# Two attentions on one core: A's first block's chain four steps sooner, exponents beside products, first scores ahead, ten block sums copied by VectorE

## The chip, the cores and the metric

The kernel runs on one core of one Trainium2 chip. The metric is the device time of one execution in microseconds. Engines are called by the names of the profile: PE is TensorE's matmul and PEld its weight load, DVE is VectorE, ACT is ScalarE, POOL is GpSimd, SP is SyncE, which issues most DMAs.

## The reference

Two attention layers with 32 heads of 18 over 2048 positions of width 576, each with its own input and weights; their outputs stand side by side.

```python
qkv = (x @ wqkv).reshape(B, S, 3, H, Dh)            # B, S, D = 1, 2048, 576; H = 32; Dh = 18
# A: each position sees the 8 positions 0, 2, .. 14 before it (masked below zero)
idx = pos[:, None] - arange(8)[None, :] * 2
logits = einsum("bhsd,bhswd->bhsw", q, kg) * scale; logits = where(mask, logits, -1e9)
a = einsum("bhsw,bhswd->bhsd", softmax(logits), vg)
# B: full attention
p = softmax(einsum("bhqd,bhkd->bhqk", q, k) * scale)
b = einsum("bhqk,bhkd->bhqd", p, v)
out = concatenate([a_heads @ wo_A, b_heads @ wo_B], axis=-1)
```

## The kernel before

**Ahead of the steps** (up to some 413 us) the inputs are split into a rounded part and a rest, so that products of 32-bit numbers can be made of rounded ones, and q, k and v of both layers are projected and stored.

**The steps.** B's attention runs in 512 steps, 8 groups of four heads (`g`) by 4 blocks of 512 queries (`b`) by 16 tiles of 128 keys (`kt`). A block thus has 16 steps, and its first has `kt == 0`. A step makes four scores of 128 keys by 512 queries (`score`, L263) into banks of the ring "scores"; ScalarE takes their exponentials (`e`, L268). The four `e` of the step before are then weighed with `v` into the bank `po` (`weigh`, L731), which also sums the denominators. The numbers of a step in the text are counted from 0.

**The maxima.** Exponentials need a bound for each query. It is found ahead of time for later blocks: query-key products of half the partitions, 512 wide (`maximum`, `take`, L160), each reduced by VectorE out of its bank (`reduce`, L168). In each step there are two whole ones and one that consists of two halves of 256 (`parts_of_maximum`: its first matmul, then, after a `nop` of ScalarE, its second). All of these use the three banks of the ring "else". `given` counts what has been handed out and `total` what there is. When all is given, the kernel goes over to weighing two steps together (`paired`).

**Row halves.** Scores and maxima use 54 to 56 of the 64 rows of one half of TensorE's array, so a score in one half runs beside a maximum in the other. The loop at the end writes the order out: first part, score 0, whole, score 2, score 1, second part, score 3, whole.

**The end of a block.** The weighing of `kt == 15` is made in the next block's first step. `finish` (L740) then copies `po` into `o`, and the next weighing waits for that copy. Normalising goes through small DMAs and GpSimd (L767 to L769) and is planned 1 to 26 steps later.

**A's attention** is made by GpSimd and VectorE beside this, in eight blocks of 256 positions, one each 54 steps (`local`, `GAP`, `A_FROM`). `plan` puts a function on the agenda of a step, and `due` emits it at that step's end. An engine runs its own queue in that order, as soon as the operands are there, so GpSimd may run ahead of or behind the step. The chain of a block: fetch q and k, `match` (GpSimd, L868 to L875, logits `lg`), `most` (VectorE, L886, three steps), `lower` (L892), `exponents` (ScalarE, L895), `total` and `inverses` (VectorE, L886 and L902), `share` (L905), `weighted` (L911 to L914), `upper`, `rest`, `put` to memory, `get` back transposed.

**A's output products.** Four for each block (`sums_of_a`, L1036): `MADE` holds the steps at whose end they are put into `inside`, and the next step makes one ahead of its last score, with two maxima woven in. ScalarE then copies one half out of its bank (L954) and VectorE adds the other (L955).

**B's output products** come at the end, in group 7 (`sum_of`, L1036, with L1055 and L1056 on VectorE). While more than four pieces of maxima are due they run inside a step like A's; later they run as `waiting` between the scores and the weighing. `producing` holds the steps with products of either kind.

**GpSimd's other work** in its queue: splitting the bounds (L103, L104 with `mh`, `mt`) and the output weights (L103, L104 with `wohi`, `wolo`), the latter three steps after each of five loads at steps 28 to 44.

Of the kernel before, what the change touches and what calls it, by code (L numbers as in the profile page):

```python
# [10 lines left out]
AF = mybir.ActivationFunctionType  # L11
# [8 lines left out]
DH = 18  # L20
# [22 lines left out]
GAP = 54  # L43

A_FROM = 10

MADE = ((88, 96, 112, 128), (144, 160, 176, 192), (201, 208, 224, 240), (250, 256, 272, 288),
        (304, 320, 336, 352), (361, 368, 384, 400), (412, 416, 432, 448), (466, 468, 475, 480))


def ap(t, *dims):

    return bass.AP(tensor=t.tensor, offset=t.offset, ap=[list(t.ap[0])] + [list(d) for d in dims])
# [8 lines left out]
def two_attentions(ctx: ExitStack, tc, xa, wa, woa, xb, wb, wob, out):  # L62
# [5 lines left out]
    nc = tc.nc  # L68
# [28 lines left out]
    po = p_po.tile([128, 512], F32, name="po")  # L97
# [10 lines left out]
    step = 0  # L108
# [99 lines left out]
    given = [0, 0]  # L208
# [17 lines left out]
    begun = deque()  # L226
# [26 lines left out]
    e_room = None  # L253
    counted = [-1]

    def score(g, b, kt, h, kind="scores"):

        assert (g, b) in placed
        qs, ks = sets[g % 3]
        p, r = divmod(h, 2)  # L260
        ps = bank(kind)
        at = slice(64 * r, 64 * r + 56)
        nc.tensor.matmul(ps, ks[at, p, 128 * kt : 128 * kt + 128], qs[at, b, p], start=True, stop=True)  # L263

        counted[0] += 1
        early = counted[0] % 8 < 6
        e = (e_room if early else work).tile([128, 512], F32, name="e", bufs=6 if early else 2)
        nc.scalar.activation(e, ps, AF.Exp, scale=SCALE)  # L268
        return e
# [100 lines left out]
    with (tc.tile_pool(name="x", bufs=1, side="right") as xp,  # L370
# [103 lines left out]
        if True:  # L474
# [34 lines left out]
            for c in range(5):  # L509
                one, other = (load, nc.scalar.dma_start) if c % 2 == 0 else (nc.scalar.dma_start, load)  # L510
# [11 lines left out]
            ahead = deque()  # L522
# [188 lines left out]
            es = []  # L711
# [10 lines left out]
        step = 0  # L722
# [13 lines left out]
    def finish(g, b):  # L736
        o = work.tile([128, 512], F32, name="o", bufs=2)
        if g == NG - 1 and b == NB - 1:
            return closing(b, o, work.tile([128, 512], F32, name="rec", bufs=1))
        nc.scalar.activation(o, po, AF.Copy)  # L740
        den = work.tile([128, 16], F32, name="den", bufs=2)
        rec = work.tile([128, 512], F32, name="rec", bufs=1)
        parts = []

        def room():
            if g == NG - 1 and b == 0:

                parts[:] = [ap(work.tile([128, 4, 128], F32R, name=f"at{i}", bufs=1), (1, 512)) for i in range(2)]
            else:
                n = work.tile([128, 2, 512], F32R, name="n", bufs=1)  # L750
                parts[:] = n[:, 0], n[:, 1], n
            return parts

        if g == NG - 1 and b > 0:
            return shortly(b, o, rec, *room()[:2])

        def store():
            if g < NG - 1:
                load(do[:, g, :, 512 * b : 512 * b + 512].rearrange("i p n -> p i n"), parts[2].bitcast(F32))
            else:  # L760
                plan(step, full(b, parts))

        for at, f in ((1, lambda: load(den, o[DH:128:32])),
                      (8, lambda: nc.vector.reciprocal(den, den)),
                      (9, lambda: load(drec[g, b].rearrange("i (p n) -> (i p) n", n=16), den)),
                      (13, lambda: load(rec, rows(drec[g, b], (512, 4), (0, 32), (1, 512)))),
                      (18, lambda: nc.gpsimd.tensor_mul(o, o, rec)),  # L767
                      (19, lambda: nc.gpsimd.tensor_copy(room()[0], o)),
                      (20, lambda: nc.gpsimd.tensor_sub(parts[1], o, parts[0])),  # L769
                      (26, store)):  # L770
            later(at, f)
# [47 lines left out]
    wo = {}  # L819

    producing = set()

    def load_wo(k, src, *pieces):

# [20 lines left out]
    def local(j):  # L845
# [20 lines left out]
        def match(c):  # L866
            pr = wide()
            nc.gpsimd.tensor_mul(pr, ap(st["q"][:, 2 * c], (SUB, 2), (0, W), (1, SUB)), window(st["k"], c))  # L868
            if c == 0:
                st["pr"] = pr  # L870
            else:
                nc.gpsimd.tensor_add(st["pr"], st["pr"], pr)  # L872
            if c == DH // 2 - 1:
                lg = st["lg"] = work.tile([128, W, SUB], F32, name="lg", bufs=1)
                nc.gpsimd.tensor_add(lg, st["pr"][:, 0], st["pr"][:, 1])  # L875
                if j == 0:
                    for w in range(1, W):
                        nc.gpsimd.memset(lg[:32, w, : DIL * w], MASKED)
# [28 lines left out]
        def weighted(c):  # L907
            if c == 0:
                st["o"] = work.tile([128, DH, SUB], F32, name="ao", bufs=1)
            at = wide()  # L910
            nc.gpsimd.tensor_mul(at, ap(st["lg"], (0, 2), (SUB, W), (1, SUB)), window(st["v"], c))  # L911
            nc.gpsimd.tensor_add(at[:, :, :4], at[:, :, :4], at[:, :, 4:])  # L912
            nc.gpsimd.tensor_add(at[:, :, :2], at[:, :, :2], at[:, :, 2:4])  # L913
            nc.gpsimd.tensor_add(st["o"][:, 2 * c : 2 * c + 2], at[:, :, 0], at[:, :, 1])  # L914
# [10 lines left out]
        def put(i):  # L925
            load(rows(dao[j, i, 0, 0], (DH * SUB, 128), (1, DH * SUB)),
                 ap(st["parts"][i].bitcast(F32), (1, DH * SUB)))
# [18 lines left out]
        def sums_of_a(h):  # L946
            his, los = zip(*wo["a"])
            w = his[:4], los[:4], his[4], los[4]
            cols = slice(288 * h, 288 * h + 288)
            if h == 0:  # L950
                st["y"] = ys["a", j, st["n"]] = work.tile([128, D], F32, name="y", bufs=4)
            one, two = beside("scores", *(halves(r, 0, w, st["x"], cols, slice(0, 128), True) for r in range(2)))
            y = st["y"][:, cols]
            nc.scalar.activation(y, two, AF.Copy)  # L954
            behind_scores.append(lambda: nc.vector.tensor_add(y, one, y))  # L955

        pieces = [(33, lower), (35, exponents), (39, share), (60, upper), (61, rest), (64, lambda: put(0)), (66, lambda: put(1))]

        pieces[:0] = [(at, lambda f=f, n=n: f(n)) for f, ats in ((most, (31, 32, 33)), (total, (36, 37, 38)),
                                                                (inverses, (38, 39))) for n, at in enumerate(ats)]  # L960
        for c in range(DH // 2):
            pieces.append((5 + 5 * c // 2, lambda c=c: match(c)))
            pieces.append((39 + 5 * c // 2, lambda c=c: weighted(c)))

        for nm, at, apart in (("q", -18, 2), ("k", -10, 2)) if j else (("q", -9, 1), ("k", -5, 1)):
            pieces += [(at + apart * i, lambda nm=nm, i=i: fetch(nm, i)) for i in range(4)]
# [77 lines left out]
    def sum_of(y, t, h, chunks, kind=None):  # L1044

        pos, cols = slice(128 * t, 128 * t + 128), slice(288 * h, 288 * h + 288)
        both = []
        for r in range(2):
            both.append([])
            for c, (hi, lo) in enumerate(chunks):  # L1050
                at = slice(64 * r, min(64 * r + 64, hi.shape[0]))
                whi, wlo = wo["b"][c]
                both[r] += [(a[at, pos], w[at, cols]) for a, w in ((hi, whi), (hi, wlo), (lo, whi))]
        one, two = beside(kind, *both)
        nc.vector.tensor_copy(y, one)  # L1055
        nc.vector.tensor_add(y, two, y)  # L1056

    def first(t, b, h):
# [74 lines left out]
    rest = NG * NB * PIECES * 2 - early  # L1133

    total = early + rest
# [4 lines left out]
    while step < ALL:  # L1140
        n, kt = divmod(step, NT)
        g, b = divmod(n, NB)
        es = [None] * 4

        whole = total - sum(given) > 1
        parts = bool(begun) or total - sum(given) > 3

        ps = bank() if inside and whole else None
        if parts:
            part = parts_of_maximum()  # L1150
        for h in (0, 2, 1, 3):

            if inside and h == 3:
                inside.pop(0)()
            es[h] = score(g, b, kt, h)
            if h == 0 and whole:
                maximum(1, ps)()
            if h == 1 and parts:
                part()
            if h == 3 and whole:  # L1160
                maximum(0)()
        for fs in (behind_scores, outside):
            while fs:
                fs.pop(0)()

        paired = paired or kt % 2 == 0 and sum(given) == total and not begun
        for _ in range(1 if paired and step < ALL - 2 else len(waiting)):
            if waiting:
                waiting.pop(0)()
        if ready and (kt % 2 == 0 or not paired):  # L1170
            weigh(ready.pop(0))
        ready.append((g, b, kt, es))
        if paired and kt % 2:
            weigh(*ready)
            ready.clear()
        due()

        if len(waiting) > (0 if not paired else 2 if kt % 2 else len(waiting)):
            waiting.pop(0)()
        step += 1  # L1180
# [24 lines left out]
```

## Time and profile before

| | us |
|---|---|
| median of 3 runs | 1619.08 |
| lowest and highest run | 1617.21, 1622.39 |
| the profiled execution's own time | 1616.82 |
| its span, first to last instruction | 1615.0 |
| mean granted TensorE clock | 0.997 of full speed |

| engine | busy us | share of the span |
|---|---|---|
| PE | 1599.0 | 99% |
| PEld | 959.5 | 59% |
| DVE | 1393.9 | 86% |
| ACT | 1212.4 | 75% |
| POOL | 961.1 | 60% |

Times of rows in the trace count from the start of the span. A row names start, duration, engine, line and operation, then the tiles (out <- in), their shapes and how many instructions are merged into it. Square brackets hold the idle time of the engine before it and what ended that time. Matmuls are pipelined, and their modelled ends overlap, so a high share of PE does not say that its array is full.

### The profile page before, as it was taken

Reading aid. Unit: us, or ns where it says so; the run is one execution under the profiler, and the core shown is the slowest. Engines: PE = TensorE matmul, PEld = TensorE weight load, DVE = VectorE, ACT = ScalarE, POOL = GpSimd, SP = SyncE. Lnnn points to the kernel's source line nnn. Section 1 sums busy time; section 2 is a strip of 40 time slices with the busy share of each in tenths; the row PEclk is TensorE's granted clock in tenths of the full one; section 3 lists DMA queues with packets and bytes.
Section 4 is the critical chain, followed back from the end, with each engine's and each line's share of the span. In section 5 each row is a group of like instructions: output and inputs, shape, how many; then the busy total and the mean of one; then the engine's idle time right before and its main releaser. Section 6 shows DMA issues by size and latency. Waiting matters only on the chain.

```text
span 1615.0 us, 35230 instructions
## 1 busy us (share of the span) xinstructions
PE 1599.0 (99%) x13394; PEld 959.5 (59%) x13394; DVE 1393.9 (86%) x2366; ACT 1212.4 (75%) x2419; POOL 961.1 (60%) x792
## 2 busy tenths in 40 slices
PE   9999999999999999999999999999999999999998
PEld 7999888999544444444444444444444444445676
DVE  5199999999899998999999999999999999999532
ACT  6424442121799998999999999999999999998444
POOL 2405742210265995996995995995996997920000
PEclk9999999999999999999999999999999999999999
DMA  8937954432222262254235235332532241034201
GB/s 250 239 121 196 275 164 133 134 104 79 60 56 64 73 147 54 62 118 113 62 85 133 72 98 115 98 91 60 125 106 58 59 135 47 22 124 139 89 38 60
DMA packets 186058, 172.11 MB, mean 107 GB/s; under 512 B 119152, under 2 KB 132976, under 8 KB 184160
## 3 DMA queue, kind: packets, MB, share of 16 engines
q1 hardware_dynamic: 181024, 158.31, 35.3%
q0 software_dynamic: 4032, 10.63, 3.1%
q8 instruction: 105, 1.72, 0.5%
q10 hardware_dynamic: 832, 0.92, 0.2%
q14 instruction: 65, 0.53, 0.1%
HBM read 96.94 MB, written 71.90 MB: 105 GB/s over the span
## 4 chain that ended last, share of the span: by engine, by line
PE 82%; POOL 7%; DVE 5%; DMA 3%; ACT 2%; issue 1%; SPq 0%; POOLq 0%; DVEq 0%; ACTq 0%
PE po L731 24%; PE bank L160 15%; PE bank L353 15%; PE bank L263 15%; PE bank L1036 8%; PE bank L290 5%; DVE mx L168 4%; ACT e L268 2%; POOL pr L868 1%; POOL pr L872 1%; POOL pr L911 1%; DMA akv<-da 1%; DMA dqk<-olo 1%; POOL pr L912 1%; POOL pr L913 0%
## 5 line engine op out<-in xcount | busy, mean ns | idle before, releaser
L168 DVE TENSOR_REDUCE mx<-bank 128x2 f32<-128x512 f32 x2048 | 1286.0, 684 | 114.5 <-PE bank L160 86.2
L268 ACT ACTIVATE e<-bank 128x512 f32<-128x512 f32 x2048 | 1050.2, 607 | 90.3 <-PE bank L263 83.2
L160 PE MATMUL bank<-ks,qs 54*128 54x256 f32 (+1 forms) x2536 | 791.8, 377 | 7.4 <-DVE mx L168 5.9
L160 PEld LDWEIGHTS bank<-ks,qs 54*128 54x128 f32 x2536 | 411.3, 184 | 464.6 <-DVE mx L168 423.4
L263 PE MATMUL bank<-qs,ks 56*128 56x512 f32 x2048 | 567.3, 426 | 0.1
L731 PE MATMUL po<-e,v 128*19 128x512 f32 x4096 | 537.9, 599 | 0.0
L263 PEld LDWEIGHTS bank<-qs,ks 56*128 56x128 f32 x2048 | 299.3, 185 | 14.7 <-issue 7.5
L868 POOL TENSOR_TENSOR pr<-aq,akv 128x1024 f32<-128x1024 f32 x72 | 158.5, 2202 | 15.4 <-DMA akv<-da 12.8
L911 POOL TENSOR_TENSOR pr<-lg,akv 128x1024 f32<-128x1024 f32 x72 | 158.5, 2201 | 0.6
L872 POOL TENSOR_TENSOR pr<-pr 128x1024 f32<-128x1024 f32 x64 | 152.6, 2384 | 5.0
L731 PEld LDWEIGHTS po<-e,v 128*19 128x19 f32 x4096 | 70.5, 97 | 129.4 <-issue 127.0
L681 ACT ACTIVATE ohi<-bank 128x512 f32<-128x512 f32 (+1 forms) x56 | 30.4, 595 | 152.5 <-issue 100.7
L353 PE MATMUL bank<-xhi,ahi 64*128 64x512 f32 (+1 forms) x448 | 113.5, 387 | 0.0
L353 PE MATMUL bank<-xhi,alo 64*128 64x512 f32 (+1 forms) x448 | 112.3, 387 | 0.0
L353 PE MATMUL bank<-xlo,ahi 64*128 64x512 f32 (+1 forms) x448 | 111.9, 388 | 0.1
L912 POOL TENSOR_TENSOR pr<-pr 128x512 f32<-128x512 f32 x72 | 92.5, 1285 | 5.6
L401 POOL TENSOR_TENSOR alo<-raw,ahi 128x512 fp32r<-128x512 f32 (+1 forms) x14 | 17.6, 1258 | 120.7 <-ACT ahi L400 88.8
L493 POOL TENSOR_TENSOR olo<-olo,ohi 128x512 fp32r<-128x512 f32 x36 | 46.2, 1294 | 66.1 <-ACT ohi L492 57.5
L767 POOL TENSOR_TENSOR o<-o,rec 128x512 f32<-128x512 f32 x29 | 37.6, 1297 | 58.7 <-ACT e L268 34.2
L103 POOL CAST mh<-mt 128x32 fp32r<-128x32 f32 x32 | 6.9, 217 | 102.3 <-DVE mt L183 99.5
L353 PEld LDWEIGHTS bank<-xhi,ahi 64*128 64x128 f32 (+1 forms) x448 | 65.0, 181 | 2.9
L353 PEld LDWEIGHTS bank<-xhi,alo 64*128 64x128 f32 (+1 forms) x448 | 63.9, 182 | 2.9
(197 smaller groups left out, 1827.6 us busy)
## 6 DMA issues: line engine op xcount, KB each, us to landing
do<-n SPq DMA_DIRECT2D x28, 512.0 KB
da<-ohi SPq DMA_DIRECT2D x52, 256.0 KB
akv<-da SPq DMA_DIRECT2D x64, 175.5 KB
out<-y SPq DMA_DIRECT2D x32, 288.0 KB
qs<-dqk SPq DMA_DIRECT2D x30, 288.0 KB
ks<-dqk SPq DMA_DIRECT2D x30, 288.0 KB
at<-dao SPq DMA_DIRECT2D x64, 128.0 KB
rec<-drec SPq DMA_DIRECT2D x29, 256.0 KB
```

Source lines behind the costliest of these rows:

```text
L160: return nc.tensor.matmul(ps if part is None else ps[:, 256 * r : 256 * r + 256], qs[at, b, p, 128 * t : 128 * t + 128], ks[at, p, 512 * k ...
L168: nc.vector.tensor_reduce(at, ps.rearrange("q (s n) -> q s n", s=2), axis=AX.X, op=ALU.max)
L263: nc.tensor.matmul(ps, ks[at, p, 128 * kt : 128 * kt + 128], qs[at, b, p], start=True, stop=True)
L268: nc.scalar.activation(e, ps, AF.Exp, scale=SCALE)
L290: nc.tensor.matmul(ps, a, b, start=c == i == 0, stop=c == 4 and i == 1)
L353: nc.tensor.matmul(ps, a, b, start=start, stop=stop)
L731: nc.tensor.matmul(po[32 * i : 32 * i + 19], vs[g][:, kt, 19 * i : 19 * i + 19], es[i], start=kt == 0, stop=kt == NT - 1)
L868: nc.gpsimd.tensor_mul(pr, ap(st["q"][:, 2 * c], (SUB, 2), (0, W), (1, SUB)), window(st["k"], c))
L872: nc.gpsimd.tensor_add(st["pr"], st["pr"], pr)
L911: nc.gpsimd.tensor_mul(at, ap(st["lg"], (0, 2), (SUB, W), (1, SUB)), window(st["v"], c))
L912: nc.gpsimd.tensor_add(at[:, :, :4], at[:, :, :4], at[:, :, 4:])
L1036: nc.tensor.matmul(ps, a, b, start=start, stop=stop)
```

## The change

`MADE` gets other steps. The chain of A's block 0 from `most` on is planned four steps sooner; `match` and the fetches stay. Where a block's exponents fall on a step of `MADE`, they are held until that product's matmuls are emitted in the next step, and stand there ahead of the copy of its half (seven blocks; block 0's are not held). In the first step of each block the first score's matmul is emitted ahead of the first part of the maximum. `finish` copies `po` on VectorE if no product stands in the next step and maxima are still due; that next step then has no part of a maximum. This applies to the ends of ten of the blocks, and ScalarE still copies at 21. B's products that run as `waiting` have their copy on ScalarE instead of VectorE.

```diff
@@ -44,8 +44,8 @@
 
 A_FROM = 10
 
-MADE = ((88, 96, 112, 128), (144, 160, 176, 192), (201, 208, 224, 240), (250, 256, 272, 288),
-        (304, 320, 336, 352), (361, 368, 384, 400), (412, 416, 432, 448), (466, 468, 475, 480))
+MADE = ((96, 99, 112, 128), (144, 153, 176, 192), (201, 207, 224, 240), (256, 261, 272, 288),
+        (304, 315, 336, 352), (362, 369, 384, 400), (416, 423, 432, 448), (466, 468, 475, 480))
 
 
 def ap(t, *dims):
@@ -253,7 +253,7 @@
     e_room = None
     counted = [-1]
 
-    def score(g, b, kt, h, kind="scores"):
+    def score(g, b, kt, h, kind="scores", between=None):
 
         assert (g, b) in placed
         qs, ks = sets[g % 3]
@@ -261,6 +261,8 @@
         ps = bank(kind)
         at = slice(64 * r, 64 * r + 56)
         nc.tensor.matmul(ps, ks[at, p, 128 * kt : 128 * kt + 128], qs[at, b, p], start=True, stop=True)
+        if between:
+            between()
 
         counted[0] += 1
         early = counted[0] % 8 < 6
@@ -737,7 +739,12 @@
         o = work.tile([128, 512], F32, name="o", bufs=2)
         if g == NG - 1 and b == NB - 1:
             return closing(b, o, work.tile([128, 512], F32, name="rec", bufs=1))
-        nc.scalar.activation(o, po, AF.Copy)
+        if step + 1 in producing or sum(given) == total:
+            nc.scalar.activation(o, po, AF.Copy)
+        else:
+
+            nc.vector.tensor_copy(o, po)
+            copied.add(step + 1)
         den = work.tile([128, 16], F32, name="den", bufs=2)
         rec = work.tile([128, 512], F32, name="rec", bufs=1)
         parts = []
@@ -819,6 +826,10 @@
     wo = {}
 
     producing = set()
+    MADE_IN = {p for ends in MADE for p in ends}
+
+    beside_product = []
+    copied = set()
 
     def load_wo(k, src, *pieces):
 
@@ -951,16 +962,22 @@
                 st["y"] = ys["a", j, st["n"]] = work.tile([128, D], F32, name="y", bufs=4)
             one, two = beside("scores", *(halves(r, 0, w, st["x"], cols, slice(0, 128), True) for r in range(2)))
             y = st["y"][:, cols]
+            while beside_product:
+                beside_product.pop()()
             nc.scalar.activation(y, two, AF.Copy)
             behind_scores.append(lambda: nc.vector.tensor_add(y, one, y))
 
-        pieces = [(33, lower), (35, exponents), (39, share), (60, upper), (61, rest), (64, lambda: put(0)), (66, lambda: put(1))]
+
+        soon = 0 if j else 4
+        in_product = A_FROM + GAP * j + 35 - soon in MADE_IN
+        pieces = [(33, lower), (35, (lambda: beside_product.append(exponents)) if in_product else exponents), (39, share), (60, upper), (61, rest), (64, lambda: put(0)), (66, lambda: put(1))]
 
         pieces[:0] = [(at, lambda f=f, n=n: f(n)) for f, ats in ((most, (31, 32, 33)), (total, (36, 37, 38)),
                                                                 (inverses, (38, 39))) for n, at in enumerate(ats)]
         for c in range(DH // 2):
-            pieces.append((5 + 5 * c // 2, lambda c=c: match(c)))
             pieces.append((39 + 5 * c // 2, lambda c=c: weighted(c)))
+        pieces = [(at - soon, f) for at, f in pieces]
+        pieces += [(5 + 5 * c // 2, lambda c=c: match(c)) for c in range(DH // 2)]
 
         for nm, at, apart in (("q", -18, 2), ("k", -10, 2)) if j else (("q", -9, 1), ("k", -5, 1)):
             pieces += [(at + apart * i, lambda nm=nm, i=i: fetch(nm, i)) for i in range(4)]
@@ -1052,7 +1069,10 @@
                 whi, wlo = wo["b"][c]
                 both[r] += [(a[at, pos], w[at, cols]) for a, w in ((hi, whi), (hi, wlo), (lo, whi))]
         one, two = beside(kind, *both)
-        nc.vector.tensor_copy(y, one)
+        if kind:
+            nc.vector.tensor_copy(y, one)
+        else:
+            nc.scalar.activation(y, one, AF.Copy)
         nc.vector.tensor_add(y, two, y)
 
     def first(t, b, h):
@@ -1143,20 +1163,21 @@
         es = [None] * 4
 
         whole = total - sum(given) > 1
-        parts = bool(begun) or total - sum(given) > 3
+        parts = (bool(begun) or total - sum(given) > 3) and step not in copied
 
         ps = bank() if inside and whole else None
-        if parts:
-            part = parts_of_maximum()
+
+        ahead = kt == 0
+        part = [parts_of_maximum()] if parts and not ahead else []
         for h in (0, 2, 1, 3):
 
             if inside and h == 3:
                 inside.pop(0)()
-            es[h] = score(g, b, kt, h)
+            es[h] = score(g, b, kt, h, between=(lambda: part.append(parts_of_maximum())) if parts and ahead and h == 0 else None)
             if h == 0 and whole:
                 maximum(1, ps)()
             if h == 1 and parts:
-                part()
+                part[0]()
             if h == 3 and whole:
                 maximum(0)()
         for fs in (behind_scores, outside):
```

## The prediction

> **What bounds the kernel now.** I read the table of stretches, then single steps in order of time, then who waited for whom.
>
> ```profile
> 800.00:900.00 100.00, 99.88 (x837) 47.12 (x836) 93.64 (x162) 94.46 (x188) 79.35 (x56) 1.00 0.43 114
> 1500.00:1615.00 115.00, 108.75 (x1213) 79.50 (x1209) 40.46 (x91) 52.45 (x104) 4.52 (x10) 0.99 0.15 57
> ...
> 511.35 1.05 PE L731 MATMUL po<-e,v 128*19 128x512 f32 x8
> 513.37 1.05 PE L731 MATMUL po<-e,v 128*19 128x512 f32 x8
> ...
> 701.50 4.07 ACT L268 ACTIVATE e<-bank 128x512 f32<-128x512 f32 x8 [0.86 <-PE bank L263]
> 701.61 3.89 DVE L168 TENSOR_REDUCE mx<-bank 128x2 f32<-128x512 f32 x6 [0.47 <-PE bank L160]
> 482.73 0.18 PEld L160 LDWEIGHTS bank<-ks,qs 54*128 54x128 f32 x1 [0.85 <-DVE mx L168]
> ```
>
> In the stretches (busy us of TensorE, its weight loads, VectorE, ScalarE, GpSimd, then granted clock) three engines are above 93% between 800 and 900 us. The weighing (L731) comes once in a step, so the distance of two of its rows is a step: 513.37 - 511.35 = 2.02 us; I use 2.03. In it ScalarE needs four exponentials, half of 4.07 = 2.03, VectorE three reductions, half of 3.89 = 1.95, and TensorE starts its first piece when a reduction frees a bank (the row with 0.85). So any extra ScalarE work, and any gap on TensorE, lengthens a step. After 1500 us the other engines are at half and less: there TensorE alone counts. The gain is to be sought in the steps longer than 2.03, one kind at a time.
>
> **The change part by part. A's first block.** One place stands out:
>
> ```profile
> 622.61 0.43 DVE L886 TENSOR_TENSOR am<-lg 128x256 f32<-128x256 f32 x1 [3.38 <-POOL lg L875]
> 623.68 0.58 PE L160 MATMUL bank<-ks,qs 54*128 54x256 f32 x1 [2.85 <-DVE mx L168]
> 624.00:631.00 7.00, 7.00 (x48) 5.04 (x48) 4.88 (x10) 2.69 (x5) 0.12 (x1) 0.57 0.17 41
> ...
> 619.78 1.05 PE L731 MATMUL po<-e,v 128*19 128x512 f32 x8
> 629.44 1.35 PE L731 MATMUL po<-e,v 128*19 128x512 f32 x8
> ...
> 1015.42 1.05 PE L731 MATMUL po<-e,v 128*19 128x512 f32 x8
> 1019.56 1.05 PE L731 MATMUL po<-e,v 128*19 128x512 f32 x8
> ```
>
> VectorE's first maximum of A's block 1 (step 95) waits 3.38 us for GpSimd's logits, the reductions queue behind it, TensorE idles 2.85 us and then runs 7 us at a mean granted clock of 0.57. Step 97, which has a product beside the copy of `po`, takes 629.44 - 619.78 = 9.66 us; its like at 1015 takes 4.14. The event costs 5.5.
>
> Is GpSimd in time after the change? From the share of block 0 to these logits it works its queue without a rest:
>
> ```profile
> 522.06 1.28 POOL L905 TENSOR_TENSOR lg<-lg,as 128x512 f32<-128x512 f32 x1 [7.07 <-ACT e L268]
> ...
> 520.09 1.05 PE L731 MATMUL po<-e,v 128*19 128x512 f32 x8
> 512.83 0.67 POOL L103 CAST wohi<-y 128x576 fp32r<-128x576 f32 x1
> 513.58 1.42 POOL L104 TENSOR_TENSOR wolo<-y,wohi 128x576 fp32r<-128x576 f32 x1
> 490.80 1.28 POOL L875 TENSOR_TENSOR lg<-pr 128x512 f32<-128x512 f32 x1
> 494.70 0.63 PE L731 MATMUL po<-e,v 128*19 128x512 f32 x4
> ```
>
> The share waits for VectorE's inverses of step 49 (weighing at 520.09). They move to step 45 (511.35): 8.7 us sooner, less 0.4 for the exponents' own lengthening, which now comes ahead of them. One split of A's output weights (0.67 + 1.42) falls behind the share instead of into the rest before it. Net 6.2 us. The asking comes sooner too: step 89 loses its product (2.06, below), and three of the block boundaries that get cheaper (0.79 each, below) lie between the share and step 95, 4.4 together. So 3.4 + 4.4 - 6.2 = 1.6 us of wait would stay; small splits that leave the stretch shorten it, and I take 1, of which TensorE sees 0.5, since it saw 2.85 of 3.38. The term is -5.5 + 0.5 = -5.0 (bounds -5.5 and -3). Block 0's own logits end at 492.1 and are masked then; step 37, which now asks for them, weighs at 494.70 and asks afterwards: over 2 us to spare, of which two cheaper boundaries take 1.6.
>
> After 2.85 us of rest the clock went down. [...]
>
> The same move puts block 0's three maxima (steps 37 to 39) beside GpSimd's splits:
>
> ```profile
> L886 DVE TENSOR_TENSOR am<-lg x8: 412/416/1306, 504.3 to 1345.0; 128x256 f32<-128x256 f32 x8
> ```
>
> Of eight first maxima (least, median, greatest ns) one took 1.31 instead of 0.42 us. Three at 0 to 0.9 give 0 to +2.7; I take +0.5, near to one in eight. [...]
>
> **Exponents beside products.**
>
> ```profile
> 515.83 1.05 PE L731 MATMUL po<-e,v 128*19 128x512 f32 x8
> 856.50 1.05 PE L731 MATMUL po<-e,v 128*19 128x512 f32 x8
> 860.41 0.41 ACT L954 ACTIVATE y<-bank 128x288 f32<-128x288 f32 x1 [0.81 <-PE bank L1036]
> 860.59 1.05 PE L731 MATMUL po<-e,v 128*19 128x512 f32 x8
> L895 ACT ACTIVATE lg<-lg x8: 633/652/655, 512.7 to 1354.1; 128x512 f32<-128x512 f32 x8
> ```
>
> Step 46, which begins behind the exponents of A's block 0, takes 515.83 - 513.37 = 2.46, 0.43 too much. A product's step takes 860.59 - 856.50 = 4.09, 2.06 too much, and in it ScalarE waits 0.81 us for the product: 0.65 us of exponents fit into that. Seven of the eight blocks move theirs there, with products drawn to those steps: 7 x -0.43 = -3.0 (bound 0, if the product's step grows by the same). Products stay 32 and cost 2.06 wherever they are. Each fetch of their operands still has eight steps or more, so the order of DMAs on SP's queue costs nothing; if one came late, TensorE would wait for it in that step.
>
> **The copy of `po` and the first score.**
>
> ```profile
> 481.74 1.05 PE L731 MATMUL po<-e,v 128*19 128x512 f32 x8
> 484.10 1.05 PE L731 MATMUL po<-e,v 128*19 128x512 f32 x8
> 486.23 1.05 PE L731 MATMUL po<-e,v 128*19 128x512 f32 x8
> 488.62 1.05 PE L731 MATMUL po<-e,v 128*19 128x512 f32 x8
> 485.55 0.63 ACT L740 ACTIVATE o<-po 128x512 f32<-128x512 f32 x1
> ...
> 483.08 0.18 PEld L263 LDWEIGHTS bank<-qs,ks 56*128 56x128 f32 x1 [0.17 <-issue]
> L263 PEldq EVENT_SEMAPHORE  x59: 51/51/51, 411.7 to 1540.6; - x59
> ```
>
> At this boundary the steps take 2.36, 2.13 and 2.39. The last two hold the copy: 0.10 + 0.36 = 0.46. In the built order ten of 31 copies go to VectorE, and the step after each leaves out the part of a maximum; so VectorE has a copy in the slot of a reduction of like size (0.65). That slot is its cover; without it the copy costs up to 0.6. Six of the ten stand in steps without a product: 6 x -0.41, with 0.05 for a worse fit. The other four lay beside a product and cost nothing there (4.14 with the copy at 1015, 4.09 without at 856); they lose that cover, 4 x +0.05. Together -2.3 (bounds -2.8 and +1).
>
> The 2.36: between the first part's weight load (482.73) and the first score's (483.08) lie 0.35 us, in which TensorE's sequencer goes through waits that are long met: eight DMA queues that loaded the block's rows, two to an instruction. The built order has them in 11 of 31 blocks. They come behind the wait for VectorE; with the score ahead they are gone through while the last weighing runs (1.05 us). The part queued behind them waits for VectorE anyway, and who waits for the part's bank sees no change. 11 x -0.33 = -3.6 (bounds -3.6 and 0; not below, as the same waits stay).
>
> **The tail.** Ten parts left out mean ten maxima later: the last is made in step 491 instead of 489.
>
> ```profile
> 1497.04 1.05 PE L731 MATMUL po<-e,v 128*19 128x512 f32 x8
> 1501.42 1.05 PE L731 MATMUL po<-e,v 128*19 128x512 f32 x8
> ...
> 1502.48 2.24 PE bank L1036 x30
> 1515.78 0.46 PE bank L263 x3
> ...
> L1055 DVE COPY y<-bank x24: 418/458/458, 1501.3 to 1599.8; 128x288 f32<-128x288 f32 x24
>   PEld bank L1036: 4.9, 15
> ```
>
> A step with maxima and a product takes 1501.42 - 1497.04 = 4.38; four scores, a product and a weighing alone 0.46 + 2.24 + 1.05 = 3.75. Two more such steps give +1.3, and step 492 is left without a product while ScalarE needs its 2.03: +0.2. Together +1.5 (bounds 0.5 and 4). The 27 copies that move from VectorE (0.46) to ScalarE (0.41, the L954 row) queue behind four exponentials, which end about when the product does: 0. Better by 0.5 at most, 0.05 of 0.46 in the 4.9 us that TensorE waited for them; worse by 2 if ScalarE is late, because the sums' additions and the next exponentials stand behind them.
>
> Sum: -5.0 + 0.5 - 3.0 - 2.3 - 3.6 + 1.5 + 0 = -11.9. The profiled execution took 1616.82, so 1604.9; the median of the runs, 1619.08, lies 2.26 above it, so 1607.2.
>
> **Rivals.** (1) GpSimd is late for block 1 as before and the clock falls again: the first term is lost, -6.9, 1612.2. For it: 1.6 us are missing by my own account. Against it: the wait was 3.38.
> (2) The steps are kept by the loop from VectorE's reduction to TensorE and back: exponents and first scores gain nothing, -11.9 + 6.6 = -5.3, 1613.8. For it: the 0.85 at each step's start. Against it: 2.46 and 2.36 stand exactly at those places.
> (3) Slower: in the tail ScalarE's 27 copies hold the banks that TensorE's next products need, queued behind exponentials whose scores came late. Lateness counts 27 times: from 0.44 us on the gain is gone, at 0.75 it is -11.9 + 20 = +8, 1627. Against it: ScalarE is busy 52.45 of 115 us there.
> (4) Nothing is left: block 0's maxima, four steps sooner, meet unfinished logits and bring the rest and the low clock to step 37, +5.5, and (2) holds too: 1619.
>
> **How the numbers follow.** Forecast 0.66, (1) 0.12, (2) 0.10, (3) 0.05, (4) 0.07. A measurement of this kernel tells about 0.3%, 4.9 us. (1) and (2) clear it narrowly, so 0.06 of theirs goes to "same" with (4): faster 0.82, same 0.13, slower 0.05. The range: with all bounds in favour (-5.5, 0, -3.0, -2.8, -3.6, +0.5, -0.5) it is -14.9, or 1604.2, and the lowest run was 1.9 under its median: 1602.0. Above it takes in (1) and most of (2): 1613.5.
>
> **What would show it.** Right: VectorE's wait for `lg` near step 95 under 1.5 us and no stretch of low clock; 4.1 us for product steps with exponents; 2.05 for the step into a block; two steps near 2.05 after it where VectorE copies; 1 to 2 us more from step 487 to 493. Wrong: a rest of TensorE over 2.5 us anywhere, product steps of 4.5, or products after 1500 us that wait for ScalarE.

## The result, and the profile after

| | before | after |
|---|---|---|
| median, us | 1617.86 (6 runs, 1615.58 to 1622.39) | 1630.94 (6 runs, 1628.68 to 1631.7) |
| ratio | | 1.0075 (95% interval 1.006 to 1.0091) |
| profiled execution, its span | 1616.82, 1615.0 | 1628.68, 1626.9 |

The changed kernel is slower by 0.75%, where 0.7% faster was forecast. Most of the steps that the prediction named did get shorter; elsewhere TensorE came to rest, and behind three of these rests the granted clock fell to 0.50 (for 10.24, 3.41 and 3.41 us).

The ledger below goes by the start of each step (its first exponential): the difference from the kernel before, in us, at steps by which both have made the same number of A's products. The columns on the right are two of the experiments told below.

| up to step | after | before + sooner + exponents | with the remedies (1608.19) |
|---|---|---|---|
| 0 | +0.7 | +1.1 | 0.0 |
| 104 | -6.5 | -4.6 | -6.9 |
| 192 | -6.8 | -4.7 | -7.0 |
| 311 | -5.4 | -4.3 | -7.2 |
| 352 | +2.8 | -4.2 | -7.7 |
| 412 | +3.5 | -0.9 | -8.2 |
| 448 | +5.8 | +0.3 | -8.6 |
| 479 | +5.1 | +0.3 | -8.8 |
| 487 | +9.7 | +0.3 | -8.8 |
| 496 | +12.9 | +0.3 | -9.2 |
| end of span | +11.9 | 0.0 | -10.0 |

At step 192 the gain is there. Most of it goes at four places: around steps 312, 420 and 479, and from 487 to 496. The table of stretches of the kernel after shows nothing of it in the middle of the loop (the same three engines above 93%) and ScalarE busier at the end (69.83 us, 52.45 before):

```profile
800.00:900.00 100.00, 99.49 (x816) 45.60 (x817) 93.26 (x161) 94.75 (x187) 78.82 (x55) 1.00 0.46 117
1500.00:1615.00 115.00, 112.73 (x1258) 80.18 (x1260) 38.23 (x77) 69.83 (x144) 4.92 (x10) 1.00 0.15 55
```

**What came as forecast.** The rows of TensorE and VectorE around the end of block 1, after:

```profile
482.06 1.05 PE L733 MATMUL po<-e,v 128*19 128x512 f32 x8
484.22 1.05 PE L733 MATMUL po<-e,v 128*19 128x512 f32 x8
486.25 1.05 PE L733 MATMUL po<-e,v 128*19 128x512 f32 x8
488.29 1.05 PE L733 MATMUL po<-e,v 128*19 128x512 f32 x8
485.50 0.68 DVE L746 COPY o<-po 128x512 f32<-128x512 f32 x1
...
1113.30 1.05 PE L733 MATMUL po<-e,v 128*19 128x512 f32 x8
1117.45 1.05 PE L733 MATMUL po<-e,v 128*19 128x512 f32 x8
```

The step into the block takes 2.16 us instead of 2.36, and with VectorE's copy (0.68) the two behind it take 2.03 and 2.04 instead of 2.13 and 2.39. A product's step that also holds exponents (1113.30 to 1117.45) takes 4.15. And the event of 5.5 us at step 97 is gone.

**What came instead**, in order of time, at A's block 5 (steps 279 and 312):

```profile
1018.35 0.46 POOL L925 TENSOR_TENSOR ao<-pr 128x128 f32<-128x128 f32 x1
1027.02 1.29 POOL L774 TENSOR_TENSOR o<-o,rec 128x512 f32<-128x512 f32 x1 [8.21 <-DMA rec<-drec]
...
1098.34 1.05 PE L733 MATMUL po<-e,v 128*19 128x512 f32 x8
1103.14 1.47 DVE L897 TENSOR_TENSOR am<-lg 128x256 f32<-128x256 f32 x1 [5.27 <-POOL lg L886]
1105.86 0.58 PE L160 MATMUL bank<-ks,qs 54*128 54x256 f32 x1 [6.46 <-DVE mx L168]
1107.65 1.91 PE L733 MATMUL po<-e,v 128*19 128x512 f32 x8
1111.29 1.05 PE L733 MATMUL po<-e,v 128*19 128x512 f32 x8
```

The stretch behind it (busy us of the engines, granted clock in the third last column):

```profile
1101.00:1112.00 11.00, 6.14 (x32) 3.00 (x32) 7.17 (x14) 3.74 (x8) 6.88 (x8) 0.53 0.29 76
```

GpSimd rests 8.21 us for the reciprocals' DMA; 80 us later its logits of block 5 come 5.27 us after VectorE asked; TensorE rests 6.46 us and then runs at half clock (0.53 over 11 us). It is the chain of the event at step 97 before, at another block: two steps of 9.31 and 3.64 us. GpSimd's work from the share of block 4 to these logits took 105.7 us instead of 97.3. The list of waits for `lg` (total us, times) says that it is not alone:

```profile
  POOL lg L886: 9.6, 5
```

Five blocks of A out of eight find VectorE waiting, where before there was one (3.4 us). At step 479 there is another kind of rest:

```profile
1482.60 0.56 SPq L773 DMA_DIRECT2D rec<-drec  x1
1483.25 2.31 SPq L195 DMA_DIRECT2D qs<-mh  x4
1485.60 2.37 SPq L195 DMA_DIRECT2D qs<-mt  x4
...
1484.89 1.05 PE L733 MATMUL po<-e,v 128*19 128x512 f32 x8
1489.25 0.46 PE L263 MATMUL bank<-qs,ks 56*128 56x512 f32 x1 [3.31 <-DMA pr<-do]
1490.53 1.91 PE L733 MATMUL po<-e,v 128*19 128x512 f32 x8
```

The first score of block 30 waits for the DMAs that bring its bounds (`qs<-mh`, `qs<-mt`): the eight semaphores that it waits for are theirs. The releaser that is named, a DMA issued at 1488.01, only came last on one of them. SyncE issued the bounds right behind a `rec`. The tail, last row of it before and first and last after (1501.42 is the first of before):

```profile
1547.32 1.91 PE L731 MATMUL po<-e,v 128*19 128x512 f32 x16
```

```profile
1511.13 1.05 PE L733 MATMUL po<-e,v 128*19 128x512 f32 x8
1560.11 1.91 PE L733 MATMUL po<-e,v 128*19 128x512 f32 x16
```

The same ten steps take 48.98 us instead of 45.90.

### The profile page after: what moved, and what is told of

It is laid out like the page before. It is cut to its first block, busy times and chain, and to the rows that moved or that the text cites. A ratio compares the mean times of both kernels' runs of the same rounds, so it can differ in the third digit from the quotient of the medians.

```text
span 1626.9 us, 35213 instructions
## 1 busy us (share of the span) xinstructions
PE 1599.4 (98%) x13386; PEld 960.5 (59%) x13386; DVE 1390.3 (85%) x2349; ACT 1219.0 (75%) x2436; POOL 960.5 (59%) x792
## 4 chain that ended last, share of the span: by engine, by line
PE 64%; POOL 20%; DMA 7%; DVE 5%; issue 2%; SPq 1%; ACT 1%; POOLq 0%; DVEq 0%; ACTq 0%
PE po L733 17%; PE bank L355 14%; PE bank L160 12%; PE bank L263 11%; PE bank L1053 6%; POOL pr L879 5%; PE bank L292 5%; POOL pr L883 4%; DVE mx L168 4%; POOL pr L922 3%; POOL pr L923 2%; DMA rec<-drec 2%; DMA drec<-den 2%; DMA dqk<-ohi 1%; POOL pr L924 1%
## 5 line engine op out<-in xcount | busy, mean ns | idle before, releaser
L355 PE MATMUL bank<-xlo,ahi 64*128 64x512 f32 (+1 forms) x448 | 117.0, 388 | 0.1
L355 PE MATMUL bank<-xhi,alo 64*128 64x512 f32 (+1 forms) x448 | 115.7, 387 | 0.0
L355 PEld LDWEIGHTS bank<-xlo,ahi 64*128 64x128 f32 (+1 forms) x448 | 67.9, 182 | 2.2 <-POOL xlo L403 0.5
```

The costliest lines, as they stand in the source:

```text
L355: nc.tensor.matmul(ps, a, b, start=start, stop=stop)
```

## The experiments

Theory G: GpSimd's stretch from the share of one block of A to the logits of the next has no reserve, and all that shortens the steps or delays GpSimd turns into rests of TensorE. Theory C: the ten VectorE copies, or the parts of maxima left out beside them, bring the rests. Both were open at first. Ratios are to runs of the kernel before on the same chip. On the three chips of the experiments its median was 1616.43, 1616.89 and 1616.21 us, so two kernels are best compared by their ratios. Dots in a code cut stand for lines or words left out.

**Less work for GpSimd.** The kernel after without one of the three additions of the weighted sums (L924, 72 times 0.74 us), so A's output is not the whole sum.

```diff
-            nc.gpsimd.tensor_add(at[:, :, :2], at[:, :, :2], at[:, :, 2:4])
```

> The changed kernel without the second of GpSimd's three folding additions in weighted (0.73 us, 72 times; A's output is then not the sum over the window). Theory GpSimd: from one block's share to the next block's logits GpSimd needs 99 us, and the 46 steps between them have become as short as that; so with 6.6 us less for each block VectorE no longer waits for lg (9.6 us in 5 waits now, then under 1), TensorE's rests at steps 258, 312, 366 and 420 (1.1, 6.5, 1.3, 1.7 us) and the low clock after step 312 go, and the time falls by about 15 us, to 1616. Theory copies (the copies on VectorE and the maxima left out make the loss): GpSimd has nothing to do with it, 1631.

Measured: 1616.7 us, ratio 1.0002 (0.9993 to 1.0012): by the ratios some 12 us less than the kernel after. The rest at step 312 falls from 6.46 to 0.86 us, though GpSimd still rests 7.85 us ahead of `o<-o,rec`. So GpSimd's lateness has that price. Two rests stay: 3.70 us at step 479, and 1.38 us at step 366, which was expected to go; ahead of it GpSimd rests 8.53 us for another `rec`, at 1160.7 us.

**Asked later.** The kernel after with A's maxima two, two and one steps later, and `lower` one step later.

```diff
-... (33, lower) ... (most, (31, 32, 33)) ...
+... (34, lower) ... (most, (33, 34, 34)) ...
```

> The changed kernel with the three maxima of A's chain planned at 33, 34, 34 instead of 31, 32, 33 and lower at 34 instead of 33; nothing else moves. Theory GpSimd: VectorE asks for the logits some 4 us later, the rests at 258, 366 and 420 go, the one at 312 shrinks from 6.5 to about 2.5 us with little or no low clock: 8 to 11 us less, 1620 to 1623. Theory copies: 1631.

Measured: 1623.8 us, ratio 1.005 (1.0032 to 1.0068). The greatest rest for A's logits is 2.43 us (step 314) instead of 6.46; step 479 rests 4.10, and the granted clock of the whole run is 0.996. Four us more for GpSimd gain 4 us by the ratios and 7.7 by the profiled spans, and something else remains.

**All copies on ScalarE**, and so no part left out.

```diff
-        if step + 1 in producing or sum(given) == total:
-            nc.scalar.activation(o, po, AF.Copy)
-        else:
-            nc.vector.tensor_copy(o, po)
-            copied.add(step + 1)
+        nc.scalar.activation(o, po, AF.Copy)
```

> The changed kernel with all 31 copies of po on ScalarE and no part of a maximum left out. Theory GpSimd: only the rest of 3.3 us at step 479 with its low clock, and the longer end of the maxima go (some 6 us), and the gain of the copies (2 us) is lost; the rest at 312 stays: 1627. Theory copies: the whole loss goes, 1618 or below.

Measured: 1614.26 us, ratio 0.999 (0.9978 to 1.0002). GpSimd's long rest, the rest at step 479 and the long tail are all gone; steps 366 and 420 keep rests of 2.03 and 1.66 us. The copies, with what hangs on them, start both large losses; G is what turns the first into time.

**A product moved back.** `MADE[3]` as before.

```diff
-... (256, 261, 272, 288),
+... (250, 256, 272, 288),
```

> The changed kernel with the product steps of A's fourth block (MADE[3]) back at 250, 256, 272, 288, so that its first half's store to memory is issued five steps sooner and not just ahead of the inverse denominators' load of B's block 16; the exponents of block 4 stand alone again. Theory GpSimd: GpSimd's rest of 8.2 us at step 279 (waiting for that load) goes, VectorE's wait at step 312 falls to under 1.5 us and the low clock goes: 9 to 10 us less, 1621 to 1622. Theory copies: 1631 or 0.4 more.

Measured: 1632.91 us, ratio 1.0102 (1.0085 to 1.012). GpSimd still rests 8.94 us ahead of `o<-o,rec`. These products and the stores behind them are not what delays this `rec`; the 9 to 10 us that were expected from them did not come.

**The copy, or the part that is left out?** First VectorE's copies with all parts kept:

```diff
             nc.vector.tensor_copy(o, po)
-            copied.add(step + 1)
```

> The kernel after with the copies of po on VectorE where it has them, but no part of a maximum left out in the step behind such a copy. Theory 1 (the parts left out let the block maxima lag, so the bounds' rows come some three steps later on SyncE's queue, rec behind them, GpSimd rests 8.21 us at step 279 and has the logits late at step 312): no rest of GpSimd over 2 us at steps 275 to 282, no rest of TensorE over 2.5 us at step 312 or 479, 1613 to 1618, the upper end if a copy and a part in one step cost 0.3 us ten times. Theory 2 (the copies on VectorE themselves are the cause): 1625 or more, with GpSimd's rest still there.

Then ScalarE's copies with the parts left out in the same steps:

```diff
-        if step + 1 in producing or sum(given) == total:
...
+        nc.scalar.activation(o, po, AF.Copy)
+        if step + 1 not in producing and sum(given) < total:
             copied.add(step + 1)
```

> The kernel after with all 31 copies of po on ScalarE, but the part of a maximum left out in the same ten steps as if VectorE had copied. Theory 1 (the parts left out are the cause): GpSimd's rest of some 8 us at step 279 and the rests of TensorE at steps 312 and 479 stay, 1626 to 1632. Theory 2 (the copies on VectorE are): none of the three, 1612 to 1617.

Measured: 1614.05 us (0.9977; 0.9967 to 0.9987) with the parts kept, 1637.94 us (1.013; 1.0113 to 1.0148) with the parts left out, above the 1632 that was expected at most. The lists of waits, SyncE for the split bounds (`L195`) and GpSimd for `rec`, in the kernel after, with the parts kept, and with the parts left out, in this order (total us, times, longest):

```profile
SPq L195 <- POOL mt L104: 14.9, 1, 14.9
POOL o L774 <- DMA rec<-drec: 8.2, 1, 8.2
```

```profile
SPq L195 <- POOL mt L104: 8.8, 1, 8.8
POOL o L773 <- DMA rec<-drec: 1.6, 1, 1.6
```

```profile
SPq L195 <- POOL mt L104: 14.9, 1, 14.9
POOL o L771 <- DMA rec<-drec: 7.6, 1, 7.6
```

The part that is left out does it; the copy on VectorE does nothing of the kind. How it does is read on GpSimd's own queue, before and after:

```profile
976.58 0.23 POOL L103 CAST mh<-mt 128x32 fp32r<-128x32 f32 x1
976.89 0.26 POOL L104 TENSOR_TENSOR mt<-mt,mh 128x32 fp32r<-128x32 f32 x1
981.84 1.29 POOL L875 TENSOR_TENSOR lg<-pr 128x512 f32<-128x512 f32 x1
```

```profile
976.88 1.28 POOL L886 TENSOR_TENSOR lg<-pr 128x512 f32<-128x512 f32 x1
978.11 0.20 POOL L103 CAST mh<-mt 128x32 fp32r<-128x32 f32 x1
978.39 0.33 POOL L104 TENSOR_TENSOR mt<-mt,mh 128x32 fp32r<-128x32 f32 x1
```

Seven parts have been left out by then. The last maximum of B's block 19 comes one step later (the transpose of its bounds runs in step 250, not 249), and their split, one place later in the order of emission, stands behind a whole piece of A's match instead of ahead of it. SyncE's queue waits for that split 14.9 us instead of 8.7, and behind it stand the loads of the next queries and keys, the `get` of A and then block 15's `drec` and `rec`. GpSimd did not take the split out of its turn: the operand was there 17 us before it ran (transpose at 960.69, split at 978.11), while GpSimd worked without a rest. The rest at step 479 (block 30's transpose in step 475 instead of 471) and the longer tail (block 31's in 492 instead of 490) go with the parts too: all five kernels here that leave parts out have them (rests of 3.3 to 4.1 us), and none that keeps them.

**The sooner chain by itself.** The kernel before with block 0's chain four steps sooner.

```diff
+        soon = 0 if j else 4
...
+        pieces = [(at - soon, f) for at, f in pieces]
+        pieces += [(5 + 5 * c // 2, lambda c=c: match(c)) for c in range(DH // 2)]
```

> The kernel before with one part of the change alone: block 0 of A asks its maxima and all that follows four steps sooner. The theory that the prediction's first term was right and only later blocks of A have no reserve expects the rest of 2.86 us at step 96 and the low clock of 6.83 us to be gone and nothing new, since from A's block 1 on every step is as it was: 5 us under the kernel before, about 1612, with VectorE idle under 0.5 us for the logits of block 1 and all later lows as before. The rival that the sooner maxima beside GpSimd's split, or the shorter loop as a whole, take the gain back expects 1615 or more and a rest of TensorE over 1 us in the loop.

Measured: 1611.51 us, ratio 0.9972 (0.9961 to 0.9983); 5.9 us less of span, all of it at step 97, and no rest over 0.8 us in the loop.

**Scalar copies and asked later**, both edits from above on the kernel after.

> The kernel after with all 31 copies of po on ScalarE, no part left out, and A's maxima asked two, two and one steps later and the lower exponents one step later. If GpSimd's stretch from the share of one block to the logits of the next, which no longer fits 46 steps, is all that the kernel with copies on ScalarE alone (1614.3) still loses, the rests of 2.03 and 1.66 us at steps 366 and 420 go and some 4 us with them: 1608 to 1611. If those rests are not GpSimd's, or the later chain only moves them, 1613 to 1617.

Measured: 1610.35 us, ratio 0.9961 (0.9947 to 0.9976). No rest over 0.45 us in the loop. That was as G expected; but 1610.35 is hardly better than the sooner chain alone, so the exponents and first scores have not brought the 6.6 us of their terms. Two more runs take them one by one.

**First scores ahead, alone**, on the kernel before.

```diff
-        if parts:
-            part = parts_of_maximum()
+        ahead = kt == 0
+        part = [parts_of_maximum()] if parts and not ahead else []
...
```

> The kernel before with one part of the change alone: in the first step of every block the first score goes ahead of the part of a maximum. The prediction's term says 11 steps fall by 0.33 us and the others stay: 3.6 us under the kernel before. What the steps of the kernels run so far suggest: every step into a block becomes 2.16 us, which takes 0.2 from the ten that were 2.36 and adds 0.14 to the eighteen that were 2.02, so the time stays within 1 us of the kernel before.

Measured: 1616.99 us, ratio 1.0001 (0.9992 to 1.001). The weighings around the steps into blocks 2 and 7, then the latter in the kernel before:

```profile
481.48 1.05 PE L733 MATMUL po<-e,v 128*19 128x512 f32 x8
483.64 1.05 PE L733 MATMUL po<-e,v 128*19 128x512 f32 x8
...
657.22 1.05 PE L733 MATMUL po<-e,v 128*19 128x512 f32 x8
659.38 1.05 PE L733 MATMUL po<-e,v 128*19 128x512 f32 x8
```

```profile
658.94 1.05 PE L731 MATMUL po<-e,v 128*19 128x512 f32 x8
660.96 1.05 PE L731 MATMUL po<-e,v 128*19 128x512 f32 x8
```

Both are 2.16 with the score ahead: 2.36 has become 2.16, but 2.02 has too. Of 30 steps into blocks nine lost some 0.19 us and eighteen grew by some 0.14; the thirty together took 64.85 us instead of 64.14. Where the 0.14 comes from shows at block 7, in the loads of the first piece and of the maximum's second part, first with the score ahead, then before:

```profile
658.20 0.18 PEld L263 LDWEIGHTS bank<-qs,ks 56*128 56x128 f32 x1 [0.85 <-ACT e L270]
658.83 0.18 PEld L160 LDWEIGHTS bank<-ks,qs 54*128 54x128 f32 x1 [0.21 <-ACTq L243]
```

```profile
659.92 0.18 PEld L160 LDWEIGHTS bank<-ks,qs 54*128 54x128 f32 x1 [0.85 <-DVE mx L168]
660.41 0.18 PEld L160 LDWEIGHTS bank<-ks,qs 54*128 54x128 f32 x1
```

The second part waits for ScalarE's `nop` (L243), and the `nop` for the part's first matmul, which now stands behind a score: 0.63 us from the first piece to the second part instead of 0.49. TensorE's loads rest 0.21 us for it instead of 0.07. At 29 of the 30 boundaries the `nop` comes 0.56 or 0.57 us behind the first piece, where the kernel before has 0.41 or 0.42.

**The sooner chain and the exponents**, with the change's `MADE`, on the kernel before.

```diff
+            while beside_product:
+                beside_product.pop()()
...
-... (35, exponents) ...
+... (35, (lambda: beside_product.append(exponents)) if in_product else exponents) ...
```

> The kernel before with two parts of the change: block 0's chain four steps sooner, and the exponents beside products with the products moved to the change's steps; copies, first scores and the tail as before. The prediction's terms: 8 us under the kernel before, 3.0 under the kernel with the sooner chain alone. The theory that a product moved off the first step of a block leaves the copy of po uncovered there (a boundary of 8.6 us without a product stands against 10.25 with one, so the product costs 1.7 there and 2.1 elsewhere): 7 times 0.43 less, 4 times 0.4 more, 1.4 us under the kernel with the sooner chain alone, about 1610.

Measured: 1616.49 us, ratio 0.9999 (0.9991 to 1.0008): 5 us over the sooner chain alone. Neither expectation held. Its share of block 5 and its asking for block 6, the products between them (ScalarE's copies, least, median and greatest ns, first and last start), and the stretch behind the asking; then the first two of the kernel before:

```profile
1118.30 1.28 POOL L907 TENSOR_TENSOR lg<-lg,as 128x512 f32<-128x512 f32 x1 [13.59 <-DVE as L904]
1220.58 0.43 DVE L888 TENSOR_TENSOR am<-lg 128x256 f32<-128x256 f32 x1 [1.92 <-POOL lg L877]
```

```profile
L958 ACT ACTIVATE y<-bank x3: 410/411/412, 1155.5 to 1212.9; 128x288 f32<-128x288 f32 x3
```

```profile
1223.00:1227.00 4.00, 4.00 (x24) 1.70 (x25) 2.75 (x7) 2.89 (x7) 1.92 (x2) 0.57 0.01 2
```

```profile
1120.87 1.28 POOL L905 TENSOR_TENSOR lg<-lg,as 128x512 f32<-128x512 f32 x1 [11.71 <-DVE as L902]
1220.77 1.28 POOL L875 TENSOR_TENSOR lg<-pr 128x512 f32<-128x512 f32 x1
1222.74 0.42 DVE L886 TENSOR_TENSOR am<-lg 128x256 f32<-128x256 f32 x1
```

```profile
L954 ACT ACTIVATE y<-bank x4: 411/412/412, 1124.9 to 1215.0; 128x288 f32<-128x288 f32 x4
```

Before, the logits end at 1222.05 and are asked for at 1222.74: 0.7 us to spare. GpSimd needs 101.2 us from the share to the logits there, 102.2 in the other. But the change moves a product from behind the share to the exponents' step, ahead of it, so three products lie in the stretch instead of four. VectorE is ready to ask 100.4 us after the share (102.28 less its wait) instead of 101.9, and 0.7 us to spare becomes a wait (1.92 here, 1.40 in the kernel after), with a rest of TensorE of 2.01 us and low clock (0.57) behind it. Of the 2.6 us between the two the product makes 1.5; the rest is GpSimd's own longer stretch, which the sooner chain alone has too (102.1 us, with a wait of 0.23). A product leaves the stretches into blocks 3, 4, 6 and 7 in this way.

**With the remedies.** Scalar copies, asked later, and the first score ahead only in twelve blocks; then the same with VectorE's ten copies and no part left out (`copied.add` taken out).

```diff
-        ahead = kt == 0
+        ahead = kt == 0 and n in (1, 2, 3, 4, 5, 20, 24, 25, 27, 28, 29, 30)
```

> The kernel after with all copies on ScalarE, no part left out, A's chain asked two steps later (1610.35 measured), and the first score ahead only in the twelve blocks whose step into the block was over 2.15 us before (1 to 5, 20, 24, 25, 27 to 30). If the first score ahead costs the other blocks 0.14 us each, 17 times 0.14 = 2.4 us less than with it everywhere: 1608. If the order costs nothing there: 1610 as before.

> As the kernel with the first score ahead in twelve blocks, but the ten copies of po beside no product on VectorE, with no part of a maximum left out. Boundaries of 8.54 us with ScalarE's copy were 8.32 with VectorE's: nine times 0.22 = 2.0 us less, 1606, if the two later steps for A keep GpSimd's logits in time; 1609 or more if VectorE's longer steps bring rests of TensorE back.

Measured: 1608.19 us (0.9948; 0.9936 to 0.9961) and 1608.15 us (0.9951; 0.9939 to 0.9964). The first is as expected, 2.2 us under the kernel with the first score ahead everywhere; the second shows no further gain, where 2.0 was expected: most of its boundaries without a product did fall, from 8.54 to some 8.35 us, but others rose by 0.25 to 0.5 (blocks 12, 13, 21, 23). The granted clock over the whole loop of the first:

```profile
440.00:1590.00 1150.00, 1147.02 (x9706) 555.30 (x9706) 1001.51 (x1717) 1059.81 (x2099) 823.21 (x632) 1.00 0.33 87
```

These two beat both the kernel before and the kernel after.

## Why the prediction was wrong, point by point

**Two steps failed.** The larger is in the term for the copies of `po`: the ten parts left out were costed at the tail alone, as "ten maxima later". With the same ten copies and all parts kept the ratio is 0.9977 instead of 1.0075, some 16 us less. The later maxima brought late bounds, a late `rec`, GpSimd's rest of 8.21 us and the rest at step 479.

The other is the question "Is GpSimd in time after the change?": it was asked for block 1 alone. The same view has the answer for the others: in blocks 2 to 7 VectorE asked 0.7 to 2.6 us after the logits were ready, with 46 steps of work between share and asking. So every 0.45 us that was taken from one of these steps went from a reserve that the sum took for endless. The two act together: with the parts left out but less work for GpSimd the ratio is 1.0002, and only with the parts kept and a later asking (0.9961 with ScalarE's copies) is no rest over 0.45 us left. It was a "rest of TensorE over 2.5 us anywhere" that the prediction named as the sign of its own failure.

- **A's first block, -5.0.** Right: -5.9 alone. GpSimd was in time to 0.02 us in the kernel after, where 1 us of wait was allowed for. That the 0.5 us of rest left to TensorE would cost no more than itself was the author's estimate, and no such rest came there; elsewhere the seven rests of 0.50 to 1.25 us in the loops of the kernels before and after had no low clock behind them.
- **Maxima beside the splits, +0.5.** Near: +0.2 with ScalarE's copies, +1.0 in the kernel after, where a first maximum took 1.41 us beside `wolo` and TensorE rested 0.99 us. Of the block's three maxima that was the only one so lengthened; the other two took 0.28 and 0.21 us.
- **Exponents beside products, -3.0.** Failed at "Products stay 32 and cost 2.06 wherever they are". The steps themselves came out as said (4.15). But with ScalarE's copy a boundary (four steps) with a product takes 10.25 us and one without 8.54, so a product costs 1.7 there and 2.1 elsewhere. Step by step against the sooner chain alone, A's blocks 1, 4 and 7, whose product came from inside a block of B, gained 0.45 to 0.47 us each, as said. A's blocks 2, 5 and 6, whose product came off the step behind a copy, gained nothing, and block 3 gained 0.33. That is 1.7 us in all. And four products leave GpSimd's stretches: the waits at A's blocks 3, 4, 6 and 7, with the low clock, cost 5.5 us.
- **Copies of `po`, -2.3.** The boundaries fell as said: 8.14 us with VectorE's copy and the part left out, 8.54 with ScalarE's. At B's blocks 10 and 20, which lost their product, they fell to 8.15 and 8.27 from 10.25 and 10.23, so the +0.05 was about right too. What was left out was the price of the part: the later maxima were already late bounds at step 250 (GpSimd's 8.21 us, then 8 us at step 312) and at B's block 30 (the rest at 479 and its low clock, 4.6).
- **First score ahead, -3.6.** Failed at the bound "not below, as the same waits stay": eighteen steps rose by 0.14. The thirty steps grew by 0.7 together, and no difference was measured. The waits are indeed gone through early. But the prediction took it that "the part queued behind them waits for VectorE anyway": its second half waits for ScalarE's `nop`, which the score ahead delays by 0.14 us.
- **Tail, +1.5.** Right mechanism, size at twice the forecast and inside its bounds: +3.1 in ten steps, with the parts left out whoever copies (48.99 us there with ScalarE's copies), and 45.36 with none left out.
- **Sums' copies on ScalarE, 0.** Better: without parts left out, steps 486 to 496 took 0.5 us less and the rest 0.7 less, -1.2 in all. Rival (3) did not happen.

Of the rivals none was this one. Rival (1) had the right mechanism at the one block where it did not occur, and the slower rival stood at the wrong engine. Left open: why leaving the parts out with ScalarE's copies costs some 7 us more than the kernel after. There the steps are longer, yet the rests at steps 258 and 366 are larger (3.49 and 2.51 us, 1.14 and 1.25 after); which part of its later bounds does that was not tried.

## What to carry to other kernels

Where a chain on a slow engine is joined to the main loop at fixed steps, read the time between "ready" and "asked" at every repetition: the smallest of them is all that the loop may be shortened by until the asking moves too. Work moved out of such a stretch shortens it as surely as a faster step does. And work that is left out "for later" can move a later link by a whole place in another engine's queue: here one step in GpSimd's cost 6 us (a wait of 14.9 instead of 8.7).

## What the runs showed of the hardware

Rests shorter than the 2.85 us of the kernel before were followed by half clock: one of 1.73 us at 1350 us in the kernel after (0.50 for 3.41 us), one of 2.01 us in the kernel with the sooner chain and the exponents (0.57 over 4 us). One of 2.03 us at the same step with ScalarE's copies was not (granted clock in the third last column):

```profile
1219.00:1229.00 10.00, 7.97 (x68) 3.69 (x65) 9.09 (x17) 7.88 (x17) 4.82 (x5) 1.00 0.06 11
```

So the length of a rest alone did not decide it. The low stretches in the loop lasted 6.83 us in the kernel before (from 623.26 us) and 10.24, 3.41 and 3.41 us in the kernel after (from 1101.06, 1350.23 and 1490.18): two, three, one and one times 3.41 us, with a granted clock of 0.50.

In the kernel after, the later switches of the clock in the loop (430 to 1600 us) lie 3, 73, 74, 114 and 115 times 3.413 us behind the first; in the kernel before there are two, twice that length apart. Of TensorE's rests of 0.5 us or more in these two loops, half clock followed those of 1.73, 2.85, 3.31 and 6.46 us, and did not follow the seven of 0.50 to 1.25 us. The ends of matmuls are modelled, so these lengths are rough; why the rests of 2.01 and 2.03 us ended differently was not shown.

Most of the price is the rest itself: at step 312 of the kernel after 8.0 us were lost with a rest of 6.46, at step 479 4.6 with one of 3.31. Yet the rests of 1.73 and 2.01 us, which lie under the 2.5 us that the prediction named as a sign of its failure, had half clock behind them too.
